# A shorter weight ring and more kept keys at the border between two decode layers

## The chip, the cores and the metric

The kernel runs on one core of a Trainium2 chip. The metric is the time of one execution on the device, in microseconds (us); three executions of the kernel before gave 2556.55, 2556.83 and 2556.87, with a median of 2556.83.

## The reference, cut to what matters

Two tokens (batch 2, one position each, model width 512) pass twice through the same pair of blocks: grouped-query attention over a cache of 32768 positions, with 32 query heads on 8 key-value heads, and a gated feed-forward block (width 1792). All is float32, and both layers use the same weights and the same caches.

```python
def _A_ref(x, k_cache, v_cache, wq, wo):
    q = (x @ wq) as [B, 32, 1, 128]
    k, v = caches, each key-value head repeated 4 times
    p = softmax(einsum("bhqd,bhkd->bhqk", q, k) * 128 ** -0.5)
    return einsum("bhqk,bhkd->bhqd", p, v) as [B, 1, 4096] @ wo

def _B_ref(x, W_gate, W_up, W_down):
    gate, up = x @ W_gate, x @ W_up
    return (gate * (gate > 0) * up) @ W_down

x = A_x
for layer in range(2):
    x = x + _A_ref(layernorm(x), k_cache, v_cache, wq, wo)
    x = x + _B_ref(layernorm(x), W_gate, W_up, W_down)
```

One key cache and one value cache are 268 MB each, and each layer needs both, so about 1.1 GB go through the core in one execution.

## The kernel before, in words

**Laps.** There are 16 groups (8 key-value heads times 2 tokens). A lap of layer 0 handles one group: its keys come as two halves of 128 x 16384 numbers (8.39 MB each), then its values as two halves. Three slots of 16384 columns in one large SBUF tensor, `arena`, take the halves in turn; they are called X, Z and Y here and begin at columns 0, 16384 and 32768. Behind them, at column `FLOW` = 49152, follow the soft-max scratch, two places for output weights, and some more. Layer 1 goes through the groups in reverse, so the group that layer 0 read last is the first that layer 1 needs.

**The border.** At the end of layer 0 the last group's second half of keys still lies in Z, its first half of values in X, its second half of values in Y. They stay for layer 1. The first half of keys does not, since the values took its slot; but its first `KEPT` = 2272 columns are copied away by GpSimd (POOL) during the last lap, to the stretch `RING[1]` to `RING[1] + KEPT`. The remaining 14112 columns are read again from HBM, in four transfers that `AGAIN` lists: two go to slot Z, as its old keys are used up, up to key block `REST` = 20 (a block is 512 columns); the other two, from block 20 on, go to ring columns that are free by then.

Between the two attentions lie the feed-forward block of layer 0 and the query projection of layer 1. Their weights pass through a **ring** that reaches from `RING[0]`, 2912 columns before `FLOW`, to `RING[1]` = `FLOW` + 4288: 7200 columns. The 2912 columns in front belong to slot Y, whose values there are moved to free PSUM banks first (the stash) and copied back later by VectorE (DVE). `ring(width)` hands out columns in order, and goes back to the start where a piece doesn't fit in what is left. The order of the pieces through it is fixed by tuples:

- one piece of output weights `wo`, 2048 columns, at `FLOW`;
- the gate and up weights `wgu` in units of 448 columns, 32 units, cut as `UNITS[0]` says: 5, 2, 4, 2, 2, 2, 2, 2, 3, 2, 2, 2, 2;
- the down weights `wd` in blocks of 512 columns, 14 blocks, cut 2, 2, 3, 3, 2, 2;
- the query weights `wq` in blocks of 512 columns, 32 blocks, cut as 4 and then fourteen times 2.

After the third query piece the first 1024 ring columns (`LENT`) are handed back to the stash (`put_back(0, LENT)`), and the ring from then on starts 1024 columns later. The 32 key blocks that still lie in Z are multiplied between the last query blocks, eight at a time.

**What sets the order.** Nothing is scheduled: the operations are recorded by a `Tape` in the order in which the code issues them, each engine runs its own in that order, and `Tape.add` works out the waits from the overlaps of regions. All transfers of weights and caches are issued by SP, one queue, in the order of `fetch`. A refill of the ring so waits until TensorE (PE) has read the last piece that overlaps its columns, and every later transfer waits behind it on SP. Every recorded instruction is emitted at one line, 214, so the profile is read by tiles: `acc`, `op`, `pair` and `small` are PSUM, `arena` the large SBUF tensor, `stat`, `qz`, `oT`, `xq` small ones.

Of the kernel before, what the change touches and what calls it, by code (L numbers as in the profile page):

```python
# [31 lines left out]
ROW = HALF * D  # L32
LANES = 16
X, Z, Y, FLOW = 0, ROW, 2 * ROW, 3 * ROW
TAIL, SPARE = 26, (32, P)
STASH = 6 * D - sum(SPARE)
LENT = 2 * D
RING = Y + ROW - STASH, FLOW + 4288
KEPT = 2272
OWN = RING[1] + KEPT  # L40
ARENA = OWN + 2 * D

# [3 lines left out]
WO = 4 * D  # L46
PART_AT = RING[1] - D, P_AT
PT_AT = WIDE_AT = OWN
# [2 lines left out]

FLOWN = (0, 16), (TAIL, 32), (16, 22), (22, 24), (24, TAIL)
ENDING = (0, 16), (16, 28), (28, 32)
REST = 20
AGAIN = (KEPT, 12 * D), (12 * D, REST * D), (REST * D, 26 * D), (26 * D, ROW)

UNITS = (5, 2, 4) + (2,) * 5 + (3, 2, 2, 2, 2), (16, 8, 8)
DOWN = (2, 2, 3, 3, 2, 2), (4, 4, 2, 2, 1, 1)
QUERY = (4,) + (2,) * 14

# [248 lines left out]
def attention_reglu_decode(nc, hold, x, k, v, wq, wo, wgu, wd, out):  # L309
# [19 lines left out]
    def tile(at, width):  # L329
        return arena[:, at : at + width]  # L330
# [7 lines left out]

    turn = [0, FLOW, 0, RING[0]]

# [7 lines left out]
    def ring(width):  # L348
        at = turn[1] if turn[1] + width <= RING[1] else turn[3]
        turn[1] = at + width  # L350
        return at
# [9 lines left out]
    def half(src, n, h, at, also=()):  # L361
        return fetch(at, src[n, h], f"slot{at // ROW}", also)
# [27 lines left out]
    def warm(width, bank=acc):  # L390

        pe.matmul(bank[:32, :width], pair, mean_cols.to_broadcast([P, width]), start=True, stop=True)
# [43 lines left out]
    def queries(L, total, first, between):  # L436
# [9 lines left out]
        for e, b in enumerate(order):  # L446
# [13 lines left out]
            if e == 1 and L > 0:  # L460
                put_back(0, LENT)
                turn[3] = RING[0] + LENT
            if kt == KT - 1:
# [16 lines left out]
    def k_blocks(lo, kt, first=0, scores=scores, cols=(0, D)):  # L480
        for at in range(-(-kt.shape[-1] // D)):
            j, ch = divmod(lo + at, 8)
            B, c = divmod(ch, 4)
            pe.matmul(scores[32 * c : 32 * c + 32, B, cols[0] : cols[1]], qz[:, 28 - 4 * j : 60 - 4 * j],
                      kt[:, at * D : at * D + cols[1] - cols[0]], start=j == first, stop=(j + 1) % NT == first)
# [56 lines left out]
    def put_back(lo, hi):  # L542
        for at, bank in stash():
            if lo <= at < hi:
                dve.tensor_copy(tile(RING[0] + at, bank.shape[-1]), bank)

# [8 lines left out]
    def feed_forward(last, total):  # L555
        xT, ss = centred(total, not last)
        gh, hT = tile(WIDE_AT, FS), tile(XT_AT, FS)
        up = acc, op
        begins = {sum(UNITS[last][:e]): n for e, n in enumerate(UNITS[last])}
        for e in range(8 * KT):  # L560
# [34 lines left out]
    for L in range(NLAYER):  # L595
# [9 lines left out]
        def keys(h, t, first=0, scores=scores):  # L605
            for e in range(0, t.shape[-1] // D, 8):
                k_blocks(h + e, t[:, e * D : min(t.shape[-1], (e + 8) * D)], first, scores)
                yield e
# [6 lines left out]
        def lap(i, second, k_first):  # L615
# [6 lines left out]
            if not last and i == NG - 1:  # L622
                pool.tensor_copy(tile(RING[1], KEPT), tile(a, KEPT))
            for _ in keys(HALF, half(k, seq[i], 1, c)):
# [21 lines left out]
        if last:  # L646
            n, e = divmod(KEPT, D)

            def again(col):
                return a + col - KEPT if col < REST * D else RING[0] + LENT + col - REST * D  # L650

# [3 lines left out]
            k_blocks(n, tile(RING[1] + n * D, e), NT // 2, gu, (0, e))  # L655
            k_blocks(n, tile(again(KEPT), D - e), NT // 2, gu, (e, D))
            for lo in range(n + 1, HALF):
                for _ in range({12: 3, REST: 2, 26: 2}.get(lo, 0)):
                    warm(448)
                if lo == REST + 4:  # L660
                    put_back(LENT, STASH)
# [65 lines left out]
```

## Time and profile before

| | |
|---|---|
| median of three runs | 2556.83 us |
| the profiled execution's own time | 2556.55 us |
| its span, first to last instruction | 2555.2 us |
| PE busy | 1335.5 us (52%) |
| VectorE busy | 157.0 us (6%) |
| ScalarE busy | 60.4 us (2%) |
| POOL busy | 18.2 us (1%) |
| SP's queue q1 | 99.9% of 16 engines' span |
| read from HBM | 1102.99 MB |
| mean granted PE clock | 0.751 |

The span runs from the first to the last instruction; 1.35 us of the execution's time lie around it. A row of the DMA issues gives what is written and read, the number of issues, the KB of each and the median us from issue to landing. A row of the timeline gives the start in us from the span's start, the us until the last of the merged instructions has ended, the engine, and what they are; for SP that is the issue alone, and the transfer runs after it. In brackets stand the idle time before and what ended it. The stretches give busy time and count for each engine, then the granted PE clock, the share of the 16 DMA engines and GB/s.

### The profile page before, as it was taken

How to read it: one execution, taken by the hardware profiler on the slowest of the kernel's cores; microseconds unless marked ns; L12 is line 12 of the kernel's file. 1: busy time of each engine (PE TensorE's matmuls, PEld its weight loads, DVE VectorE, ACT ScalarE, POOL GpSimd, SP SyncE). 2: the span in 40 equal slices, each digit the busy share in tenths (PEclk: the TensorE clock that was granted, in tenths of full speed). 3: DMA queues.
4: the chain of work that ended last, by engine and by line, in shares of the span. 5: the costliest groups of instructions: out<-in, count | busy, mean ns of one | idle time of the engine just before them, and what ended most of it. 6: DMA issues, size and time to landing. Idle time of an engine off the chain costs nothing.

```text
span 2555.2 us, 20572 instructions
## 1 busy us (share of the span) xinstructions
PE 1335.5 (52%) x9542; PEld 366.1 (14%) x9542; DVE 157.0 (6%) x409; ACT 60.4 (2%) x82; POOL 18.2 (1%) x25
## 2 busy tenths in 40 slices
PE   4554545455444554455586554455445554455456
PEld 1111111111111111111121111111111111111112
DVE  1000000000000000000111000000000000000001
ACT  0000000000000000000000000000000000000000
POOL 0000000000000000000000000000000000000000
PEclk9677777777777777777798777777767777777778
DMA  9999999999999999999999999999999999999999
GB/s 425 429 440 429 427 441 430 440 430 431 436 430 440 430 438 429 430 440 430 425 423 440 434 435 432 431 435 435 434 433 431 436 433 435 432 432 435 433 435 389
DMA packets 27248, 1103.29 MB, mean 432 GB/s; under 512 B 3033, under 2 KB 3169, under 8 KB 8033
## 3 DMA queue, kind: packets, MB, share of 16 engines
q1 hardware_dynamic: 27216, 1103.06, 99.9%
q8 instruction: 12, 0.20, 0.0%
q14 instruction: 4, 0.02, 0.0%
q10 hardware_dynamic: 16, 0.00, 0.0%
HBM read 1102.99 MB, written 0.07 MB: 432 GB/s over the span
## 4 chain that ended last, share of the span: by engine, by line
DMA 73%; PE 26%; issue 0%; SPq 0%; DVE 0%; ACT 0%; ACTq 0%
DMA arena<-k 37%; DMA arena<-v 34%; PE acc L214 12%; PE pair L214 11%; DMA arena<-wd 1%; PE small L214 1%; PE op L214 1%; DMA arena<-wq 1%; DMA arena<-wgu 1%; SPq L214 0%; DVE stat L214 0%; DVE arena L214 0%; DVE xq L214 0%; ACT arena L214 0%; ACTq L295 0%
## 5 line engine op out<-in xcount | busy, mean ns | idle before, releaser
L214 PE MATMUL acc<-arena 128*16 128x512 f32 (+2 forms) x4288 | 612.1, 726 | 531.8 <-DMA arena<-v 522.0
L214 PE MATMUL pair<-arena,qz 128*32 128x512 f32 x4098 | 590.7, 730 | 557.5 <-DMA arena<-k 557.5
L214 PEld LDWEIGHTS pair<-arena,qz 128*32 128x32 f32 x4098 | 151.5, 131 | 987.0 <-issue 697.2
L214 PEld LDWEIGHTS acc<-arena 128*16 128x16 f32 (+1 forms) x4288 | 136.8, 112 | 970.6 <-issue 595.5
L214 ACT ACTIVATE arena<-pair,stat 128x1024 f32<-128x1024 f32 x32 | 35.7, 1114 | 2388.1 <-DVE stat L214 2388.1
L214 DVE TENSOR_SCALAR arena<-acc,stat 128x512 f32<-128x512 f32 (+1 forms) x39 | 25.5, 667 | 1051.3 <-PE acc L214 1051.3
L214 DVE TENSOR_REDUCE stat<-pair 128x1 f32<-128x1024 f32 x32 | 39.2, 1225 | 633.5 <-PE pair L214 633.5
L214 DVE STREAM_TRANSPOSE arena<-arena 128x512 f32<-128x512 f32 (+1 forms) x68 | 43.4, 674 | 40.8 <-ACT arena L214 40.7
L214 PE MATMUL small<-stat,cst 128*128 128x1 f32 (+1 forms) x72 | 16.6, 300 | 48.7 <-ACT arena L214 48.7
L214 PE MATMUL small<-arena,cst 128*128 128x32 f32 x64 | 13.1, 286 | 51.6 <-DVE arena L214 51.6
L214 PEld LDWEIGHTS small<-cst,arena 128*128 128x128 f32 x264 | 32.1, 191 | 28.7 <-issue 27.0
L214 PE MATMUL small<-cst,arena 128*128 128x4 f32 x264 | 35.0, 256 | 0.5 <-DVE arena L214 0.5
L214 PE MATMUL op<-arena,oT 128*2 128x512 f32 (+1 forms) x312 | 34.4, 526 | 0.4 <-DVE oT L214 0.3
L214 DVE MEMSET oT<- 128x8 f32 x33 | 2.1, 65 | 513.4 <-PE op L214 513.4
L214 POOL COPY arena<-arena 128x2048 f32<-128x2048 f32 (+1 forms) x7 | 13.5, 1923 | 2191.2 <-PE op L214 2046.7
L214 PE MATMUL op<-arena 128*32 128x448 f32 (+1 forms) x128 | 22.7, 573 | 3.0 <-DMA arena<-wq 1.4
L214 PEld LDWEIGHTS small<-stat,cst 128*128 128x128 f32 x72 | 13.6, 236 | 56.9 <-ACT arena L214 52.2
L214 PEld LDWEIGHTS small<-arena,cst 128*128 128x128 f32 x64 | 9.5, 188 | 80.5 <-DVE arena L214 80.5
L214 ACT ACT_TABLE_LOAD x16 | 20.5, 1283 | 11.4 <-DMA xq<-x 11.1
L214 PE MATMUL acc<-cst 128*32 128x448 f32 (+1 forms) x48 | 18.3, 480 | 0.0
L214 PE MATMUL small<-cst,stat 128*128 128x2 f32 x8 | 1.7, 286 | 18.6 <-DVE stat L214 18.1
L214 PE MATMUL small<-arena 128*32 128x128 f32 x224 | 9.0, 277 | 3.1 <-DVE arena L214 1.7
(63 smaller groups left out, 98.6 us busy)
## 6 DMA issues: line engine op xcount, KB each, us to landing
arena<-wo SPq DMA_DIRECT2D x6, 2048.0 KB, 31.5
arena<-v SPq DMA_DIRECT2D x2, 4096.0 KB, 37.4
arena<-wq SPq DMA_DIRECT2D x14, 512.0 KB, 6.4
arena<-wgu SPq DMA_DIRECT2D x10, 448.0 KB, 6.7
arena<-wo SPq DMA_DIRECT2D x4, 1024.0 KB, 25.3
arena<-wgu SPq DMA_DIRECT2D x1, 3584.0 KB, 44.6
arena<-wgu SPq DMA_DIRECT2D x2, 1792.0 KB, 48.9
arena<-v SPq DMA_DIRECT2D x2, 1536.0 KB, 41.3
```

The source lines that it names most:

```text
L214: ins = getattr(engine, op.call)(*args, **op.kw)
```

## The change

The ring loses 448 columns at its end (6752 instead of 7200), and the kept keys gain them at their front: they reach from `FLOW` + 3840 to the same end as before, `FLOW` + 6560. So 2720 columns are copied by POOL, and 13664 columns are read again instead of 14112. `REST` moves from block 20 to 21, so that what goes to ring columns still fits them. The first piece of gate weights has 4 units instead of 5 (with the 2048 columns of `wo` ahead of it, it again ends with the ring), and two later pieces have 3 units each, where before one had 3; there are 13 pieces in both.

```diff
-RING = Y + ROW - STASH, FLOW + 4288
-KEPT = 2272
+RING = Y + ROW - STASH, FLOW + 3840
+KEPT = 2720
 OWN = RING[1] + KEPT
 ...
-REST = 20
+REST = 21
 AGAIN = (KEPT, 12 * D), (12 * D, REST * D), (REST * D, 26 * D), (26 * D, ROW)

-UNITS = (5, 2, 4) + (2,) * 5 + (3, 2, 2, 2, 2), (16, 8, 8)
+UNITS = (4, 2, 4, 2, 2, 2, 3, 3) + (2,) * 5, (16, 8, 8)
 DOWN = (2, 2, 3, 3, 2, 2), (4, 4, 2, 2, 1, 1)
 QUERY = (4,) + (2,) * 14
```

How the program's order moves is shown at three places, as differences (- before, + changed), with the waits of each instruction in brackets. `tensor_done` is PE's semaphore, `vector_done` VectorE's. On SP, from the output weights of layer 0 to the down weights:

```order
 L214 DMA arena<-wo 128x2048 [waits vector_done]
-L214 DMA arena<-wgu 128x2240 [waits tensor_done]
+L214 DMA arena<-wgu 128x1792 [waits tensor_done]
 L214 DMA arena<-wgu 128x896 [waits tensor_done,vector_done]
 L214 DMA arena<-wgu 128x1792 [waits tensor_done,vector_done]
+L214 DMA arena<-wgu 128x896 [waits tensor_done] x3
+L214 DMA arena<-wgu 128x1344 [waits tensor_done] x2
 L214 DMA arena<-wgu 128x896 [waits tensor_done] x5
-L214 DMA arena<-wgu 128x1344 [waits tensor_done]
-L214 DMA arena<-wgu 128x896 [waits tensor_done] x4
 L214 DMA arena<-wd 128x1024 [waits tensor_done] x2
```

The first piece is 448 columns shorter, and the two of 1344 columns come right after the third of the small ones. Also on SP, from the query weights to the half of keys behind the reload:

```order
 L214 DMA arena<-wq 128x2048 [waits tensor_done]
 L214 DMA arena<-wq 128x1024 [waits tensor_done] x14
-L214 DMA arena<-k 128x3872 [waits tensor_done]
-L214 DMA arena<-k 128x4096 [waits tensor_done]
-L214 DMA arena<-k 128x3072 [waits tensor_done]
+L214 DMA arena<-k 128x3424
+L214 DMA arena<-k 128x4608 [waits tensor_done]
+L214 DMA arena<-k 128x2560 [waits tensor_done]
 L214 DMA arena<-k 128x3072
 L214 DMA arena<-k 128x16384 [waits tensor_done]
```

The sizes of the reload move, and its first transfer has no wait of its own any more: the last query piece ahead of it waits for a PE instruction that stands behind the keys it overwrites. On VectorE, in layer 1's query projection, where `COPY arena<-pair` is the stash being copied back to the first 1024 ring columns:

```order
 L214 TENSOR_SCALAR stat<-small 128x2 [waits tensor_done]
 L214 TENSOR_SCALAR stat<-stat 128x2 [waits gpsimd_done]
-L214 COPY arena<-pair 128x512 [waits tensor_done] x2
+L214 COPY arena<-pair 128x512 x2
 L214 STREAM_TRANSPOSE arena<-op 128x512 [waits tensor_done]
 L214 TENSOR_SCALAR qT<-arena,stat 128x4x4 [waits vector_done] x2
```

Its wait is gone: the query piece that lay on these columns stands elsewhere now, and a piece of down weights that PE has long read is there instead.

## The prediction

> **What bounds the kernel now.** I read the page first, for which resource is never free, then the stretches around the border between the two layers, where all edits lie, and then the issue and landing of single transfers there.
>
> ```profile
> span 2555.2 us, 20572 instructions
> DMA  9999999999999999999999999999999999999999
> q1 hardware_dynamic: 27216, 1103.06, 99.9%
> HBM read 1102.99 MB, written 0.07 MB: 432 GB/s over the span
> DMA 73%; PE 26%; issue 0%; SPq 0%; DVE 0%; ACT 0%; ACTq 0%
> arena<-k SPq DMA_DIRECT2D x62, 39.2
> arena<-v SPq DMA_DIRECT2D x60, 29.7
> ```
>
> One queue, SP's, keeps the 16 DMA engines occupied for 99.9% of the span; no slice is below 9. The chain of waits alternates between landings and the PE work that follows them; but PE, half idle, is not what fills the span: the bytes are. The last two rows say how far ahead the steady laps run: a half of a key or value cache (16384 columns, 8.39 MB, 19.4 us at 432 GB/s) is issued 29.7 to 39.2 us before it lands, 10 to 20 us more than its own transfer. So whatever shifts the queue in the border shifts everything behind it by as much, and the end too.
>
> ```profile
> core 0: us, PE busy (x) PEld busy (x) DVE busy (x) ACT busy (x) POOL busy (x), PEclk, DMA share, GB/s
> 400.00:1000.00 600.00, 302.35 (x2136) 80.78 (x2128) 29.39 (x73) 17.42 (x21) 3.79 (x2) 0.74 1.00 433
> 1272.00:1324.00 52.00, 43.42 (x374) 14.11 (x370) 11.79 (x38) 0.63 (x1) 1.26 (x2) 1.00 1.02 419
> ```
>
> The first stretch is steady laps, the second the border from the first gate weights to the last query weights. Even there the DMA share is 1.02: the queue does not run dry, although PE waits there for small pieces and those wait for ring columns that PE gives back. It only moves 419 GB/s instead of 433, with pieces of 448 to 1120 KB in place of 8 MB. So the border is bound by bytes as well, with a second condition close behind: each refill of the ring has to be issued early enough.
>
> **Part one: fewer bytes.** Of the first keys of layer 1, 448 columns more lie in the arena already and are not read again: 448 x 128 x 4 = 229,376 bytes, at 432 GB/s 0.53 us (0.55 at 419). The reload stays four transfers (3424, 4608, 2560, 3072 columns for 3872, 4096, 3072, 3072). The gate weights keep 13 transfers and their bytes (4+2+4+2+2+2+3+3+2x5 = 32 units), so what small pieces cost in rate costs the same: nothing added. The border's 3% below the laps' rate over 52 us is 1.6 us for some 35 transfers, 0.05 us each; no count changes.
>
> **Part two: the longer copy** on POOL, 2720 columns for 2272.
>
> ```profile
> 1221.22 2.08 POOL L214 COPY arena<-arena 128x2272 f32<-128x2272 f32 x1 [144.41 <-DMA arena<-k]
> 1232.59 2.94 SPq L214 DMA_DIRECT2D arena<-v  x6
> ```
>
> In proportion 2.08 us becomes 2.49, ending at 1223.7. Only the value load into the same slot waits for it, and that load is held until 1232.6 by PE anyway, which reads the slot too: 8.9 us of cover, cost nothing. Were PE not there, it would cost 0.41 us of that load's lead.
>
> **Part three: the shorter ring.** Here lies the price, since each refill is issued later against the data ahead of it. Three kinds of rows measure it: how soon pieces are issued now, how soon they land, and how little a transfer needs.
>
> ```profile
> 1314.30 7.71 SPq L214 DMA_DIRECT2D arena<-wq  x7
> arena<-wq SPq DMA_DIRECT2D x7, 512.0 KB, 6.3
> 1311.84 0.33 SPq L214 DMA_DIRECT2D arena<-wq  x1
> arena<-wq SPq DMA_DIRECT2D x1, 512.0 KB, 6.3
> ```
>
> Seven query pieces are issued over 7.71 us, the last taking 0.33, so one every 1.23 us, each when PE has used up the piece six before it: with the first 1024 ring columns given back for the stash, 7200-1024 = 6176 columns hold six pieces of 1024. With 6752-1024 = 5728 they hold five. The change thus takes not 448 columns but a whole piece from this loop: a refill then has 6.3-1.23 = 5.07 us until it is due, of which 1.21 is its own transfer (524,288 bytes), 3.9 us to spare.
>
> The turn before is tighter. Now the first query piece (2048 columns) ends at ring column 7168, six more follow from the start, and the seventh, issued at 1311.84, is the first to wait for the first. In the changed ring the sixth piece of wd wraps to column 0, the first query piece stands at 1024 to 3072, the next three up to 6144, and a further 1024 don't fit: the fifth wraps onto the first. It can't be issued before 1311.84 either, since PE uses the first piece no earlier (all bytes up to there are the same), but it is due two places earlier than the seventh, at 1311.84+6.3-2x1.23 = 1315.7. That leaves 3.84 us, less 1.21 for the transfer: **2.6 us to spare**, the least anywhere. Queued behind it on SP is every later query piece, and PE waits for those.
>
> Two other refills wait for later readers through the wrap:
>
> ```profile
> 1298.22 0.33 SPq L214 DMA_DIRECT2D arena<-wd  x1
> arena<-wd SPq DMA_DIRECT2D x1, 768.0 KB, 7.4
> 1300.41 0.33 SPq L214 DMA_DIRECT2D arena<-wd  x1
> 1302.70 0.33 SPq L214 DMA_DIRECT2D arena<-wq  x1
> arena<-wq SPq DMA_DIRECT2D x1, 1024.0 KB, 8.0
> 1304.46 0.33 SPq L214 DMA_DIRECT2D arena<-wq  x1
> ```
>
> The fourth piece of wd waits for unit 30 of the gates instead of 27; the piece that waits for unit 30 today goes out at 1300.41. Due at 1298.22+7.4 = 1305.6, it keeps 5.2 us, less 1.8 for 768 KB: 3.4 to spare. The first query piece waits for block 5 of wd instead of 3, at 1304.46 by the row of the one that waits for it today; due at 1310.7, it keeps 6.2, less 2.4 for 1 MB: 3.8.
>
> How much must be spare? No row shows a refill that came too late, so I bound it:
>
> ```profile
> out<-xq SPq DMA_DIRECT2D x1, 64.0 KB, 1.5
> arena<-wq SPq DMA_DIRECT2D x1, 21.9
> arena<-wgu SPq DMA_DIRECT2D x1, 448.0 KB, 5.5
> ```
>
> From below: the output with nothing ahead of it took 1.5 us for 64 KB (0.15 us of transfer), so 1.35. The very first load, 8.39 MB with nothing ahead, took 21.9, 2.5 more than the 19.4 of its bytes. From above: the tightest refill of the border as it stands, a gate piece, landed 5.5 us after its issue, 1.06 of them its transfer, so 4.4 spare were enough. The nearest row is the first load, HBM to the arena on the same queue: 2.5 us, just under the 2.6. I take no stall, and keep 1.35 to 4.4 for the range. The Trainium skill, page "DMA: Bandwidth & Descriptors", section "Anatomy of one DMA", gives a fit, made on another issue path, of about 2.0 us plus the bytes at 436 GB/s per transfer, mostly the confirmation of the last write. By it the fifth query piece would be ready 3.2 us after issue, inside its 3.84, and the sum stays; no run yet shows that figure in a busy queue.
>
> At 4.4 the stalls would be 4.4-2.6 = 1.8 there, 1.0 and 0.6 at the two pieces above, 0.5 in each of two further rounds of five, and about as much again where the last query piece waits behind the kept keys: some 5 us, before the saved 0.53 is taken off.
>
> **Part four: the end of the reload.** The keys' second region moves from block 20 to block 21, so the next half (16384 columns into the same slot) is issued one block later.
>
> ```profile
> 1337.62 1.92 PE L214 MATMUL pair<-arena,qz 128*32 128x512 f32 x16 [0.52 <-DMA arena<-k]
> 1339.60 0.33 SPq L214 DMA_DIRECT2D arena<-k  x1
> 1344.91 1.48 PE L214 MATMUL pair<-arena,qz 128*32 128x512 f32 x10 [0.24 <-DMA arena<-k]
> ```
>
> Eight blocks (16 instructions) take 1.92 us, so the ninth adds 0.24, and the second piece ends 64 columns (0.08 us) later: issue at about 1339.9. The last piece lands, by the PE row that waits for it, at about 1344.7 now and 0.53 sooner then: 4.2 to 4.3 us of queue remain where 5.1 stand now, still above the 2.5. Cost nothing; at a need of 4.4, 0.1 to 0.2. The extra kept block and the other split of one block (160+352 for 224+288 columns) are PE work that replaces as much, under a PE that waits for keys again at 1337.62 (0.52 us).
>
> **Sum.** The profiled execution took 2556.55 (span 2555.2 and 1.35 around it); minus 0.53 gives 2556.02. The median of the three runs, 2556.83, lies 0.28 above that execution, so I forecast **2556.3 us**.
>
> **Rivals.** A: *the ring runs dry.* If a refill in the busy queue needs over 2.6 us beyond its transfer, the queue idles first at the fifth query piece, then at the other places. For it: one query piece in six is gone from the loop. Against: the first load's 2.5. It breaks even with 0.53 us of stall, a need of about 3.1, and is slower from there. At 3.5 there is 0.9 at the first place, 0.1 at wd and about 0.5 at the last query pieces: 1.5, net +1.0, 2557.8; at 4.4 net about +4.4, 2561.2, which is still inside the 0.2%.
>
> B: *the saving is swallowed*, equal time, 2556.8: at the end of the reload the next half comes as much later as the data ahead ends sooner. It needs a latency that eats the 4.2 us left there, or PE and DVE work between the last keys and the soft-max becoming the bound. Against: the laps' 10 us of lead.
>
> C: *the border gains more than the bytes*, since the larger gate pieces (3 and 3 units) move faster: at most two transfers' worth of the 0.05 us, 2556.2; no different result.
>
> **How the numbers follow.** Forecast 0.68 (its own range 2555.8 to 2556.8, the runs' spread of 0.3 on both sides), A 0.18, B 0.10, C and the unnamed 0.04. The range for eight in ten takes in the forecast, B, the lower half of A up to a need near 4, and a little for a session whose base is another: 2555.2 to 2558.8. What a measurement of this kernel can tell from no change is 0.2%, 5.1 us. Every case but an A beyond its bound lies inside: same 0.97, slower 0.02, faster 0.01.
>
> **What would show it.** HBM read 0.23 MB less, 1102.76. The query pieces of the loop land about 5.1 us after issue instead of 6.3, the fifth about 3.8, still 1.23 apart, and the DMA share of the border stays at 1.02. The copy takes about 2.5 us and no SP wait ends on it. The half issued at 1339.60 goes out near 1339.9, and the last reload ends at 1344.2. I am wrong if the fifth query piece lands more than 4 us after its issue and PE's wait for query weights grows there, or if the stretch after the border starts no earlier than before.

## The result and the profile after

The changed kernel takes 2561.42 us (median of 21 runs, 2559.97 to 2564.73) where the kernel before takes 2556.76 (21 runs, 2556.42 to 2557.13). The ratio is 1.0019, with a 95% interval of 1.0013 to 1.0025: it is **slower by 4.7 us**, 0.19%, a little under the 0.2% that I had called the edge of "no change", but well clear of no difference. The runs also scatter more, over 4.8 us instead of 0.7. The forecast was 2556.3, with a range up to 2558.8.

The profiled execution took 2560.97 us, its span 2559.7. The lines of the page of the changed kernel that answer to those of before:

```profile
span 2559.7 us, 20572 instructions
DMA  9999999999999999999999999999999999999999
q1 hardware_dynamic: 27216, 1102.84, 99.9%
HBM read 1102.76 MB, written 0.07 MB: 431 GB/s over the span
L214 PE MATMUL op<-arena 128*32 128x448 f32 (+1 forms) x128 | 21.7, 573 | 5.4 <-DMA arena<-wq 3.1
L214 PE MATMUL small<-arena 128*32 128x128 f32 x224 | 9.0, 277 | 5.0 <-DMA arena<-wd 3.2
```

The bytes fell as the change says, by 0.23 MB. The queue still counts as occupied for 99.9%. But PE's query and down products now wait longer for their weights; before, the same two groups read:

```profile
L214 PE MATMUL op<-arena 128*32 128x448 f32 (+1 forms) x128 | 22.7, 573 | 3.0 <-DMA arena<-wq 1.4
L214 PE MATMUL small<-arena 128*32 128x128 f32 x224 | 9.0, 277 | 3.1 <-DVE arena L214 1.7
```

The last number of each row is the idle time that its main releaser ended: 3.1 us for query weights instead of 1.4, and 3.2 for down weights where the down products' main wait had been for DVE. The steady laps of the kernel before stand in the prediction, at 433 GB/s. Two later stretches of it are the end of layer 0 with the gates, then the down and query weights. The changed kernel's rows below are the laps and the same two:

```profile
1260.00:1296.00 36.00, 31.41 (x242) 9.13 (x242) 6.90 (x21) 0.63 (x1) 0.56 (x1) 0.96 1.00 417
1296.00:1324.00 28.00, 23.23 (x217) 7.90 (x218) 5.58 (x18) 0.00 (x0) 0.70 (x1) 1.00 1.02 421
```

```profile
400.00:1000.00 600.00, 307.33 (x2136) 81.91 (x2132) 29.39 (x73) 17.41 (x21) 3.79 (x2) 0.73 1.00 433
1260.00:1296.00 36.00, 31.41 (x242) 9.23 (x242) 6.90 (x21) 0.63 (x1) 0.56 (x1) 0.94 0.99 412
1296.00:1324.00 28.00, 19.50 (x185) 6.14 (x182) 4.92 (x15) 0.00 (x0) 0.70 (x1) 1.00 0.99 372
```

The laps move 433 GB/s in both. Most of the loss lies in the last 28 us: 372 GB/s instead of 421, at a DMA share that only goes from 1.02 to 0.99. At 421 GB/s the 1.37 MB that are missing there take 3.3 us, of the 4.5 by which the span is longer. This is the first thing to learn from this trace: **the DMA share hardly showed the queue running short; the GB/s beside it did.** Stretches of 4 us, and of half a microsecond within the last of them, show it more sharply (changed kernel):

```profile
1300.00:1304.00 4.00, 2.68 (x40) 1.10 (x40) 1.61 (x4) 0.00 (x0) 0.00 (x0) 1.00 1.03 393
1308.00:1312.00 4.00, 2.57 (x39) 1.49 (x38) 0.66 (x4) 0.00 (x0) 0.00 (x0) 1.00 0.93 359
1314.00:1318.00 4.00, 3.38 (x14) 0.64 (x14) 1.52 (x4) 0.00 (x0) 0.70 (x1) 1.00 0.85 279
1314.50:1315.00 0.50, 0.50 (x4) 0.00 (x0) 0.00 (x0) 0.00 (x0) 0.43 (x1) 1.00 0.80 229
1315.00:1315.50 0.50, 0.42 (x4) 0.14 (x4) 0.20 (x2) 0.00 (x0) 0.27 (x1) 1.00 0.84 164
```

The trace also holds every packet of the queue. In the border of the kernel before, between 1296 and 1324 us, each of the 2025 packets of 4 KB takes 159 ns; in the changed kernel some take up to 1246 ns. The first 512 KB behind an empty queue, in a run further down, begin in the same way (up to 1181 ns). This reads as DMA engines that ran out of work and, when they start again, count as busy through such long packets, which keeps the share up while the rate falls.

The worst stretch, 279 GB/s, begins with the issue of the fifth query piece. Its rows, and PE's wait for it:

```profile
1314.01 0.33 SPq L214 DMA_DIRECT2D arena<-wq  x1
arena<-wq SPq DMA_DIRECT2D x1, 512.0 KB, 5.6
1316.58 1.05 PE L214 MATMUL op<-arena 128*32 128x512 f32 x4 [0.17 <-DMA arena<-wq]
1319.68 1.05 PE L214 MATMUL op<-arena 128*32 128x512 f32 x4 [2.05 <-DMA arena<-wq]
```

It landed 5.6 us after its issue, where by the prediction it had 3.84 until it was due. PE, which waited 0.17 us for the piece ahead of it, waited 2.05 for this one. The two other pieces that the prediction had named as tight, the fourth of wd and the first of the queries:

```profile
1300.91 0.33 SPq L214 DMA_DIRECT2D arena<-wd  x1
arena<-wd SPq DMA_DIRECT2D x1, 768.0 KB, 6.1
1305.34 0.33 SPq L214 DMA_DIRECT2D arena<-wq  x1
arena<-wq SPq DMA_DIRECT2D x1, 1024.0 KB, 7.5
```

The wd piece took 6.1 us where it had 5.2, the query piece 7.5 where it had 6.2. Beyond their transfers (1.2, 1.8 and 2.4 us), the three were 4.4, 4.3 and 5.1 us under way. Part of such a time is spent behind the piece ahead, so a second measure stands beside it: how long after the landing of the piece ahead a piece lands, less its own bytes at 420 GB/s. I call this its lateness. In the border of the kernel before it stays under 0.2 us for every piece. In the changed kernel it is 1.9 us for the fifth query piece and 0.55 for the fourth of wd. It is nothing for the first query piece, which lands 2.45 us behind its forerunner (2.65 before) and only inherits the delay. Three pieces that the prediction had not named as tight are late as well: the third of wd by 0.3 us, the sixth of wd by 0.9 and the thirteenth of the queries by 0.7. The sixth of wd, with PE's wait for it, first in the kernel before and then in the changed one:

```profile
1308.10 0.65 PE L214 MATMUL small<-arena 128*32 128x128 f32 x16 [0.42 <-DMA arena<-wd]
```

```profile
1302.76 0.33 SPq L214 DMA_DIRECT2D arena<-wd  x1
arena<-wd SPq DMA_DIRECT2D x1, 512.0 KB, 7.7
1310.46 0.65 PE L214 MATMUL small<-arena 128*32 128x128 f32 x16 [1.37 <-DMA arena<-wd]
```

It was issued 5.5 us before the piece ahead of it landed, so it was not issued late. All latenesses of the border add up to 4.6 us; the span is 4.5 longer, with 0.5 us of bytes saved. So rival A came about, with a time near its upper end (2561.2 us), though not at all of its places and at some others.

### The profile page after: what moved, and what is told of

It is laid out like the page before. It is cut to its first block, busy times and chain, and to the rows that moved or that the text cites. A ratio compares the mean times of both kernels' runs of the same rounds, so it can differ in the third digit from the quotient of the medians.

```text
span 2559.7 us, 20572 instructions
## 1 busy us (share of the span) xinstructions
PE 1341.6 (52%) x9542; PEld 365.2 (14%) x9542; DVE 157.0 (6%) x409; ACT 60.3 (2%) x82; POOL 18.5 (1%) x25
## 3 DMA queue, kind: packets, MB, share of 16 engines
q1 hardware_dynamic: 27216, 1102.84, 99.9%
HBM read 1102.76 MB, written 0.07 MB: 431 GB/s over the span
## 4 chain that ended last, share of the span: by engine, by line
DMA 73%; PE 26%; issue 0%; SPq 0%; DVE 0%; ACT 0%; ACTq 0%
DMA arena<-k 37%; DMA arena<-v 34%; PE acc L214 12%; PE pair L214 11%; DMA arena<-wd 1%; PE op L214 1%; PE small L214 1%; DMA arena<-wq 1%; DMA arena<-wgu 0%; SPq L214 0%; DVE stat L214 0%; DVE arena L214 0%; DVE xq L214 0%; ACT arena L214 0%; ACTq L295 0%
```

## The experiments

Three theories stood at the start. **Theory 1**: refills of the shorter ring are issued too late, a refill in the busy queue needing some 4.0 to 4.4 us beyond its transfer. **Theory 2**: the longer copy, the odd reload sizes or the kept keys themselves cost it. **Theory 3**: the cut of the gate weights. The table gives medians of ten runs (21 for the changed kernel), each against the kernel before on the same chip (2556.76 us for the first row, 2556.91 for the second recut and the ring of 7648, 2556.73 and 2556.75 for the others):

| kernel | ring / kept | us | against before | ratio, 95% interval |
|---|---|---|---|---|
| changed kernel | 6752 / 2720 | 2561.42 | +4.7 | 1.0019 (1.0013 to 1.0025) |
| ring alone | 6752 / 2272 | 2562.07 | +5.3 | 1.0021 (1.0011 to 1.0031) |
| changed, lent columns later | 6752 / 2720 | 2559.76 | +3.0 | 1.0011 (1.0001 to 1.0020) |
| ring 7136 | 7136 / 2336 | 2558.90 | +2.2 | 1.0009 (0.9999 to 1.0018) |
| ring 7168 | 7168 / 2304 | 2557.33 | +0.6 | 1.0003 (0.9993 to 1.0013) |
| before, five in the loop | 7200 / 2272 | 2557.61 | +0.9 | 1.0002 (0.9993 to 1.0012) |
| before, four in the loop | 7200 / 2272 | 2560.57 | +3.8 | 1.0014 (1.0005 to 1.0024) |
| changed, first recut | 6752 / 2720 | 2558.59 | +1.8 | 1.0007 (0.9998 to 1.0017) |
| changed, second recut | 6752 / 2720 | 2557.11 | +0.2 | 1.0002 (0.9992 to 1.0011) |
| before, recut larger | 7200 / 2272 | 2557.43 | +0.7 | 1.0003 (0.9994 to 1.0013) |
| ring 7648 | 7648 / 1824 | 2557.33 | +0.4 | 1.0002 (0.9992 to 1.0011) |

Seven of the eleven intervals take in 1, so those differences are not shown by the medians alone. What is said of them below rests on the order among the kernels and on the traces.

**The ring alone.** The changed kernel with the old number of kept columns at their old place, so that 448 columns lie idle:

```diff
 RING = Y + ROW - STASH, FLOW + 3840
-KEPT = 2720
-OWN = RING[1] + KEPT
+KEPT = 2272
+OWN = FLOW + 6560
+KEPT_AT = OWN - KEPT
 ...   # KEPT_AT for RING[1] where the kept keys are written and read
```

> The ring of the change (6752 columns, its cuts of the gate weights, second region from block 21) with the old 2272 kept columns; 448 columns of the arena lie unused, and nothing is left out of the computation. Theory 1 (refills of the shorter ring come too late): all of the loss and none of the saved bytes, so the change's 4.7 us and 0.5 more: about 5.2 us over the kernel before, 2562.0. Theory 2 (the longer copy, the odd reload sizes or the other kept keys cost it): the loss goes, at most 1 us over before. Theory 3 (the gate cut itself): 4.7 to 5.2 as well; the next runs tell it from theory 1.

Measured 2562.07, as theory 1 said. The copy and the kept keys of theory 2 are out: with the old ones the loss is still there. It is 0.65 us larger, near the 0.53 of the bytes, but both kernels scatter over more than 4 us. The reload keeps most of its new sizes here, since `REST` stays at 21; the second recut below clears them, which has the changed kernel's whole reload and loses 0.2 us.

**The fifth query piece.** The hand-back of the lent columns moves from behind the third query piece to behind the fifth, so that the fifth piece no longer lies on the first:

```diff
-            if e == 1 and L > 0:
+            if e == 2 and L > 0:
                 put_back(0, LENT)
                 turn[3] = RING[0] + LENT
```

> The changed kernel, with the first 1024 ring columns handed back one query block later, so that the fifth query piece goes onto them (over down weights that PE has long read) and no longer waits for the first query piece. Theory 1: the 1.9 us that this piece came late go, the sixth piece has then about 3.8 us and loses up to 0.5: 1.0 to 1.5 us below the changed kernel, about 2560.1. Theories 2 and 3: no difference to the changed kernel, 2561.4.

Measured 2559.76, 1.7 us below the changed kernel, slightly more than expected. PE's timeline of this kernel shows that the wait is gone from its place, while a later piece is late instead:

```profile
1315.76 4.82 PE L214 MATMUL op<-arena 128*32 128x512 f32 x20
1320.82 1.05 PE L214 MATMUL op<-arena 128*32 128x512 f32 x4 [0.25 <-DMA arena<-wq]
1323.39 1.05 PE L214 MATMUL acc<-arena 128*32 128x512 f32 x4 [1.51 <-DMA arena<-wq]
```

**Whole pieces or columns.** Two kernels 32 ring columns apart, both with the changed gate cut; one holds five query pieces beside the lent columns, the other just six:

```diff
-RING = Y + ROW - STASH, FLOW + 4288      # 7200
-KEPT = 2272
+RING = Y + ROW - STASH, FLOW + 4224      # 7136; FLOW + 4256 in the other
+KEPT = 2336                              # 2304
 ...
-REST = 20
+REST = 21                                # 20
```

> Ring of 7136 columns and 2336 kept, that is 64 columns moved instead of 448, with the changed cut of the gate weights and the second region from block 21. 7136 less the lent 1024 hold five query pieces (6112 of 6144 columns needed for six). Theory 1, read as whole pieces: 2 to 3 us over the kernel before, although the ring is only 64 columns shorter. Read as columns: 64/448 of the loss, 0.7 us. Theory 2: near nothing. Theory 3: 4.7 us.

> Ring of 7168 columns and 2304 kept: 32 columns more in the ring than the run beside it, and just enough for six query pieces (6144 columns). Same cut of the gate weights; second region from block 20. Theory 1, as whole pieces: the query pieces keep their lead and only the gate cut's worse fit is left, 0 to 1 us over the kernel before, so 2 us below the run with 7136. As columns: 0.3 us below it at most. Theory 3 (the gate cut): 4.7 us over before.

Measured 2558.90 and 2557.33: 1.6 us for 32 columns, which are 0.04 us of bytes. That is most of what a whole piece was expected to cost and far from what columns would. The ten runs of the two overlap (2557.53 to 2562.24 and 2556.86 to 2558.97), and `REST` differs too, but the lateness in the first one's profiled execution lies at query pieces (the first, the seventh and the thirteenth), ahead of the reload. Theory 3 is out too, since the gate cut of the change costs at most some 0.6 us in the second kernel.

**The loop by itself.** The kernel before, with the ring's last 1024 or 2048 columns closed to the query pieces once the lent ones are handed back; nothing else moves:

```diff
-    turn = [0, FLOW, 0, RING[0]]
+    turn = [0, FLOW, 0, RING[0], RING[1]]
 ...
-        at = turn[1] if turn[1] + width <= RING[1] else turn[3]
+        at = turn[1] if turn[1] + width <= turn[4] else turn[3]
 ...
-                turn[3] = RING[0] + LENT
+                turn[3], turn[4] = RING[0] + LENT, RING[1] - 1024   # 2048 in the other
```

> The kernel before, with its 7200 columns, kept columns and cuts, where the query pieces may not use the ring's last 1024 columns once the lent ones are handed back: five pieces of 1024 stand in the loop instead of six, and nothing else moves. Theory 1 (a refill in the busy queue needs 4.0 to 4.4 us beyond its own transfer, as the late ones of the changed kernel showed): 3.9 are left in the loop, 3.2 at the last query piece: 0.1 to 0.5 in each of two rounds and about 1 at the end, 1 to 2 us over before, 2557.8 to 2558.8. Rival 2 (an idle queue's 1.35 to 2.5 us suffice and the loss comes from the shorter ring in another way, such as the kept columns or the gate cut): no difference, 2556.8.

> The same with 2048 columns taken from the query pieces: four in the loop. Theory 1: each round is 1.2 us shorter than with five, so 2.6 us are left where 4.0 to 4.4 are needed: 1.4 to 1.8 in each of three rounds and more at the last piece, 5 to 6.5 us over before, about 2562.5. With an idle queue's 1.35: no difference; with its 2.5: none either, or some tenths.

Measured 2557.61 and 2560.57. The direction is theory 1's, the sizes lie below it: 0.9 of an expected 1 to 2 us, 3.8 of 5 to 6.5. PE's timeline says why. Five in the loop first, then four:

```profile
1317.00 1.05 PE L214 MATMUL op<-arena 128*32 128x512 f32 x4 [0.18 <-DMA arena<-wq]
1318.24 1.05 PE L214 MATMUL op<-arena 128*32 128x512 f32 x4 [0.19 <-DMA arena<-wq]
1319.46 1.05 PE L214 MATMUL acc<-arena 128*32 128x512 f32 x4 [0.16 <-DMA arena<-wq]
...
1327.00 0.62 PE L214 MATMUL acc<-arena 128*32 128x512 f32 x2 [0.79 <-DMA arena<-wq]
```

```profile
1317.12 1.05 PE L214 MATMUL op<-arena 128*32 128x512 f32 x4 [0.22 <-DMA arena<-wq]
1318.36 1.05 PE L214 MATMUL op<-arena 128*32 128x512 f32 x4 [0.19 <-DMA arena<-wq]
1320.51 1.05 PE L214 MATMUL acc<-arena 128*32 128x512 f32 x4 [1.09 <-DMA arena<-wq]
1321.94 0.62 PE L214 MATMUL acc<-arena 128*32 128x512 f32 x2 [0.38 <-DMA arena<-wq]
```

With 3.9 us of spare (five pieces) most refills come in time, and one in the row does not. With 2.6 (four), a late piece stops PE for 1.09 us, and some of the refills behind it are late again. So a need of 4.0 to 4.4 is not what every refill takes. Nor is it a bound above which none is late, as the sixth wd piece of the changed kernel showed. The landings of the border's refills in all 13 profiled executions, from the second gate piece to the last query piece, say it in numbers. Call the time from a refill's issue until the piece ahead of it lands its lead; in the loop of five it is 3.8 to 3.9 us, about the spare reckoned above. Late means here by more than 0.3 us:

| lead | refills | late |
|---|---|---|
| under 3.5 us | 14 | 7 |
| 3.5 to 4.5 us | 91 | 19 |
| 4.5 to 6 us | 231 | 8 |
| over 6 us | 93 | 0 |

The eight of the third row stand in executions in which an earlier refill had a lead under 4 us. In the three executions whose leads never fell below 4.3 us (the kernel before, the ring of 7648, and the one with the empty queue) no refill was late. The latenesses of an execution also add up to about what it loses: 1.3 us with five in the loop and 4.0 with four, whose spans are 1.2 and 4.4 us longer than before. With the saved bytes counted in, sum and loss agree within 0.7 us in all but two executions (ring 7136 and the recut with larger pieces, off by 1.1 and 1.3). What decides whether a refill with a short lead is late is not shown. That it differs from run to run would fit the wider scatter of the slow kernels.

**The same ring, cut to fit.** The changed ring and kept columns, with all weights cut otherwise, once with the aim of a fitting ring and once also with an eye on the phase in which the kept keys are multiplied. The filler of PE that the expectations name is matmuls whose results nothing uses:

```diff
-UNITS = (4, 2, 4, 2, 2, 2, 3, 3) + (2,) * 5, (16, 8, 8)
-DOWN = (2, 2, 3, 3, 2, 2), (4, 4, 2, 2, 1, 1)
-QUERY = (4,) + (2,) * 14
+UNITS = (4, 3, 3, 2, 2, 2, 1, 3, 3, 2, 2, 2, 3), (16, 8, 8)
+DOWN = (2, 2, 1, 3, 2, 3, 1), (4, 4, 2, 2, 1, 1)
+QUERY = 4, 1, 3, 3, 1, 1, 2, 1, 1, 2, 1, 2, 1, 1, 2, 2, 2, 1, 1
 ...
-            if e == 1 and L > 0:
+            if e == 2 and L > 0:
 ...
-            if c in ((4, 8) if last else (4, 7, 10)):
+            if c in ((4, 8) if last else (4, 8, 10)):
```

> The changed kernel's ring (6752) and kept columns (2720), with the pieces cut so that every refill can be issued at least 4.3 us plus its transfer before it is due by my reckoning from the waits: gates 4,2,2,2,4,2,2,4,2,2,3,3; down 1,2,2,1,3,3,2; queries 4,3,4,2,2,1,1,2,1,2,2,2,2,2,1,1; the lent columns handed back one query block later, and PE's filler after other down blocks. Theory 1: nearly all of the loss goes, 2556.4 to 2557.5, because pieces fit and not because the ring is longer. Theory 2 (the columns, the copy, the reload): it stays near the changed kernel's 2561.4.

> The changed kernel's 6752 ring columns and 2720 kept ones, all weights in pieces that fit the ring and spread the refills: gates 4,3,3,2,2,2,1,3,3,2,2,2,3; down 2,2,1,3,2,3,1; queries 4,1,3,3,1,1,2,1,1,2,1,2,1,1,2,2,2,1,1; lent columns handed back one query block later; PE's filler after other down blocks. By the waits, most refills have 4.3 us or more beyond their transfer. Theory 1: 2557 to 2558.5, well under the changed kernel's 2561.4, some tenths of it from more and smaller pieces. Theory 2 (the columns, the copy, the reload cost it): 2561 or more.

The diff is the second one's. The first one's output is wrong: its fourth query piece lies on the lent columns, and these are filled back while half of it is unread, so that PE multiplies values of the last group in place of one block of query weights. The transfers and the amount of work are still those of the edit. Measured 2558.59 and 2557.11: the first still loses 1.8 of the 4.7 us, more than expected, the second 0.2, inside its interval. So the shorter ring does not cost 4.7 us by itself; the places where its pieces wrap do. Where the second spends the saved bytes is not separated: its profiled execution (2557.66) has two late query pieces, 0.65 and 1.5 us, and it also moves more and smaller pieces.

**Larger pieces in the old ring.**

```diff
-UNITS = (5, 2, 4) + (2,) * 5 + (3, 2, 2, 2, 2), (16, 8, 8)
-DOWN = (2, 2, 3, 3, 2, 2), (4, 4, 2, 2, 1, 1)
-QUERY = (4,) + (2,) * 14
+UNITS = (5, 2, 4, 4, 2, 4, 4, 3, 4), (16, 8, 8)
+DOWN = (2, 2, 3, 2, 3, 2), (4, 4, 2, 2, 1, 1)
+QUERY = 4, 4, 3, 2, 3, 2, 2, 3, 2, 3, 2, 1, 1
 ...
-            if c in ((4, 8) if last else (4, 7, 10)):
+            if c in ((4, 8) if last else (4, 7, 9)):
```

> The kernel before (7200 columns, 2272 kept) with fewer and larger pieces that still leave each refill 4.4 us: gates 5,2,4,4,2,4,4,3,4; down 2,2,3,2,3,2; queries 4,4,3,2,3,2,2,3,2,3,2,1,1; filler of PE after other down blocks. Theory 1: no refill late; larger pieces move a little faster, 0.3 to 0.5 us under the kernel before, 2556.3. If a need above 4.4 holds for large pieces: up to 1 us over.

A miss: 2557.43, 0.7 over the kernel before instead of 0.3 to 0.5 under it; its ten runs spread from 2556.78 to 2560.43. My reckoning, by which each refill had 4.4 us at least, was wrong: the profiled execution, the slowest of the ten, has leads down to 3.4 us. A gate piece with 3.5 landed 1.6 us late, and a later query piece with 4.8 landed 2.1 late. No version here beats the kernel before.

**An idle queue.** The kernel before, whose very first load is cut in two:

```diff
-            whole, begins = fetch(Y, wq, f"slot{Y // ROW}"), {}
+            fetch(Y, wq[:, : 2 * D])
+            fetch(Y + 2 * D, wq[:, 2 * D :], f"slot{Y // ROW}")
+            whole, begins = tile(Y, ROW), {}
```

> The kernel before, whose very first load is cut into 1024 columns (512 KB, as large as a query piece of the border) and the rest. Nothing is ahead of it in the queue, though more follows. If an idle queue needs about 1.35 us beyond the transfer's 1.2, it lands 2.6 us after issue; if the 2.5 that the prediction read from the 8 MB load are true of any load, 3.7; if the 4.0 to 4.4 of the late refills hold in an idle queue too, 5.2 to 5.6, and the busy queue is not the reason. The time itself stays: 2556.8.

One run, 2557.15 us. The piece, first in the queue:

```profile
arena<-wq SPq DMA_DIRECT2D x1, 512.0 KB, 3.9
```

3.9 us, or 2.7 beyond its transfer. So the prediction read the idle queue rightly from the 8 MB load (2.5). The same 512 KB took 5.6 us when they were issued into the border's queue as the fifth query piece.

**The other way.** 448 columns more in the ring, 448 fewer kept:

```diff
-RING = Y + ROW - STASH, FLOW + 4288
-KEPT = 2272
+RING = Y + ROW - STASH, FLOW + 4736
+KEPT = 1824
 ...
-UNITS = (5, 2, 4) + (2,) * 5 + (3, 2, 2, 2, 2), (16, 8, 8)
+UNITS = (6, 2, 4) + (2,) * 10, (16, 8, 8)
```

> The opposite of the change: 448 columns more in the ring (7648) and as many fewer kept (1824), the first piece of gate weights with 6 units. Theory 1: the kernel before loses nothing to late refills, so a longer ring brings nothing and 229,376 more bytes cost 0.53 us: 2557.3. If the kernel before lost time to late refills as well, it comes out equal or faster, 2556.8 or less. Theory 2 (kept columns cost): faster, 2552 to 2556.

Measured 2557.33, 0.4 us over before: about the price of the bytes, though inside the interval of no change. A longer ring brings no gain, and no refill is late in the trace of the kernel before, so that kernel loses nothing measurable to late refills.

## Why the prediction was wrong, point by point

- **What bounds the kernel**: right. The bytes set the time wherever refills are early: moving 229,376 bytes measured 0.4 us one way (ring of 7648) and 0.65 the other (ring alone), against 0.53; the second lies between two kernels that scatter over 4 us.
- **Fewer bytes**: right in size (HBM read fell to 1102.76 MB, as forecast), but lost in the rest.
- **The longer copy**: right. It took 2.45 us of the 2.49 forecast, and the run with the old copy kept the whole loss:

```profile
1221.50 2.45 POOL L214 COPY arena<-arena 128x2720 f32<-128x2720 f32 x1 [145.74 <-DMA arena<-k]
```

- **The shorter ring**: the places named, their order and the whole query piece that the loop loses were right. (Only five pieces, not six, follow the first query piece from the ring's start; the seventh of all, which the reckoning uses, is the first to wait for it.) One place was overlooked: the third piece of wd waits for units 26 and 27 of the gates instead of 24 and 25, and came 0.3 us late. What failed is the term "I take no stall": a need of 2.5 us beyond the transfer, chosen because the first load was the nearest row. It was nearest in kind, not in state: nothing was ahead of it. With nothing ahead 512 KB need 2.7; the fifth query piece, issued 2.5 us before the piece ahead of it landed, took 4.4 and came 1.9 us late. Of the rows at hand only the other bound, from a gate piece in that same busy queue, told of it.
- **The sum at that other bound**, 4.4 us, was 2561.2, and measured are 2561.4. That they agree so closely is partly luck. At the fifth piece it had 1.8 us against 1.9 measured, but at the two other tight pieces 1.0 and 0.6 against 0.55 and nothing, and 1.2 us came at two wd pieces for which it had no term. A single need that every refill has is not what the runs show.
- **The cross-check at 2.0 us**: this fixed cost is what the Trainium skill gives (page "DMA: Bandwidth & Descriptors", section "Anatomy of one DMA"), fitted on another issue path. An estimate from it has the fifth piece ready in 3.2 us, which spoke for no stall too. The runs show 3.9 with nothing ahead and 5.6 in the busy queue, and the measurement decides.
- **The border's DMA share of 1.02 as the sign that the queue has reserve**: wrong as a measure. The share stayed at 1.03 in a stretch that moved 393 GB/s, where the kernel before moved 426.
- **The end of the reload**: small, as said. The next half went out later by the border's delay, 1345.60 instead of 1339.60, and landed 5.3 us later than before. One microsecond of that is won back at the half behind it; the other 4.2 us stay through all of layer 1 to the end, as the prediction held that any shift there would be carried.
- **What would show it**: the sign "the fifth query piece lands more than 4 us after its issue" came as written. The loop's forecast of 5.1 us held roughly for the pieces behind the ninth (5.3 to 6.0 us); the sixth to the ninth took 6.5 to 7.2, behind the late fifth piece. The half issued at 1339.60 was to go out near 1339.9 and the last reload to end at 1344.2; they came at 1345.60 and 1349.9, with the border's delay.
- **The rivals**: A happened. I had given it 0.18, on the strength of one row that was taken in another state of the queue. B and C, both without late refills, did not.

## What to carry to other kernels

In this kernel a ring of refills costs by whole pieces and by where they wrap, not by its columns: before a buffer is cut, count for each refill which reader it waits for and how much data stands ahead of it. Take the time that a refill needs from the same queue under the same load, and where only a bound exists there, let the sum stand on that bound and not on a quieter row. Behind refills with short leads, some were late here that had time enough. Judge whether a DMA queue has reserve by its GB/s against the best stretch of the same kernel and by the shortest lead of a refill, not by its busy share.

## What the runs showed of the hardware that was not expected

A 512 KB load needed 3.9 us from issue to landing with nothing ahead of it, and 5.6 us when it was issued into this busy queue 2.5 us before PE could begin with the piece ahead of it (1314.01 and 1316.58 in the rows above). The DMA engines' busy share hardly fell meanwhile (0.99 over 28 us, at 372 GB/s instead of 421), because packets of 4 KB that otherwise take 159 ns took up to 1246. And a late refill is no matter of one threshold: with leads of 3.8 to 3.9 us in the loop of five most refills came in time and one kept PE waiting for 0.79 us, while in the first recut of the shorter ring a query piece with a lead of 2.5 us landed in time. A kernel just short of reserve shows it in its scatter (4.8 us over 21 runs against 0.7) as well as in its median.
